# Two heads of q and k in one tile: scores as three products over the row halves of the array

## The chip, the cores and the metric

The kernel runs on one NeuronCore of a Trainium2 chip. The metric is the device time of one execution in microseconds (us), the median of several runs. The engines are TensorE (PE in the profile, its weight loads PEld), VectorE (DVE), ScalarE (ACT), GpSimd (POOL) and SyncE (SP), which issues the DMAs.

## The reference

Three stages follow each other: attention with a sigmoid in place of softmax, a Fourier mixing with an FFN, and a gated convolution with two projections. The change touches the first alone, and of it the scores.

```python
batch, n_heads, seq, head_dim = (4, 12, 448, 64)
...
scale = 1.0 / np.sqrt(q.shape[-1])
scores = scale * np.matmul(q, k.transpose(0, 1, 3, 2)) - np.log(S)
attn = 1.0 / (1.0 + np.exp(-scores))
return np.matmul(attn, v).astype(np.float32)
```

Then x = the heads side by side (4 x 448 x 768); u = x + real(fft2(x)), normalised; u + relu(un @ w_ch1) @ w_ch2; then sigmoid(causal convolution) * (x @ w_val) @ w_out. Everything is float32.

## The kernel before

**Scores in two parts.** q and k are split into an upper part of fewer mantissa bits (`qh`; F32R, a rounded float32 that TensorE takes in one pass) and the rest (`ql`). The scores of a head are (kh + kl)(qh + ql) or that without kl ql. D = 64 rows are only half of the array's 128, so before, a tile `ks` holds kh in one half of its rows and kl in the other, and q lies twice in its tile, in both halves; one product with `qh` and one with `ql` give all four terms. `upper` makes the upper part on VectorE (L308) or ScalarE (L310), `prep_q` and `prep_k` the rest on GpSimd (L317, L324). `ON_V = 24` says until when `upper` is on VectorE: all of batch 0, later only the k of odd heads.

**Steps.** Heads go in pairs, 6 pairs in a batch and 24 in all, and a pair in four steps, t = 4i .. 4i + 3 (s = t % 4), over 128 keys each. 448 keys are three tiles of 128 and 64 left over; in the step s = 3 the 64 left over of both heads stand in one tile of 128 columns, so it fills one score tile instead of two. The four `ks` tiles are used in turn, and the keys of odd heads are rolled by 64 with 64 zero columns beside them for that step.

**Order.** The program is written out in the order in which it is issued; each engine takes its instructions in that order. A step t issues `scores(t + 1)`, `sigmoid(t)` (ScalarE, L378), the preparation `prep(t + 6)` and loads, then pieces of background work taken from queues (the Fourier mixing of the batch before, its normalisation, the FFN's weights, which VectorE turns from float64 to float32 from L172 on and splits), then `values(t - 1)`:

```python
if s < 3:
    for h in range(2):
        hs = slice(64 * h, 64 * h + 64)
        nc.tensor.matmul(p[hs, :S], v[:, s, hs], a[:, h], start=(s == 0), stop=False)
else:
    nc.tensor.matmul(p[:, :S], v[:, s], a[:, 0], start=False, stop=True)
```

For s < 3 these are two products that each use 64 columns of the array (L390), for s = 3 one whole product (L392). `ps_s` (two buffers) holds scores, `sg` the sigmoids. L399 copies a finished pair to `acc`. The FFN and the rest (from `up` on) follow the attention stage; L745, L768 and so on are their products.

Of the kernel before, what the change touches and what calls it, by code (L numbers as in the profile page):

```python
# [7 lines left out]
F32 = mybir.dt.float32  # L8
F32R = mybir.dt.float32r
# [3 lines left out]
AF = mybir.ActivationFunctionType  # L13
ALU = mybir.AluOpType
# [29 lines left out]
W_RATE = (1.6, 0.25, 1.25)  # L44
FFN_RATE = (0.8, 2.2, 2)
PACE = 3
ON_V = 24
POOL_BATCHES = (2, 3)
ABSMAX = bass.bass_isa.ReduceOp.absmax
LEAST = 2.0 ** (896 // 8 - 127)  # L50
# [12 lines left out]
def body(tc, qd, kd, vd, w1d, w2d, cwd, wvd, wod, cdd, k12d, csd, eyed, out):  # L63
    nc = tc.nc
    V, A, P = nc.vector, nc.scalar, nc.gpsimd

    def pool(stack, name, side="left"):
        return stack.enter_context(tc.tile_pool(name=name, bufs=1, side=side))
# [219 lines left out]
    cs = fk.tile([128, 2, 2, 3, NP], F32R, name="cs")  # L288
    e16 = fk.tile([76, 2, 2, NE], F16, name="e16")
    V.memset(e16, 0.0)  # L290
    NHEAD, NHALF, NPAIR = B * H, 2 * B * H, B * NT
    raw, qk, st_of = {}, {}, {}
    kst = [wk.tile([128, 512], F32R, name=f"ks{i}") for i in range(4)]
    for i in range(4):
        P.memset(kst[i][:, (S, 0)[i % 2]:][:, :64].bitcast(F32), 0.0)
    SLOT = 1

    def load_qk(i):
        b, j, side = i // H, i % H // 2, i % 2
        k = wk.tile([64, S], F32, tag="k", bufs=3, name="k")  # L300
        q = wk.tile([128, S], F32, tag="q", bufs=3, name="q")
        nc.sync.dma_start(out=q, in_=qd[b, j, side])
        nc.sync.dma_start(out=k, in_=kd[b, j, side])
        raw[i] = q, k

    def upper(out, in_, m):
        if m != 2 and (m < ON_V or m % 4 == 3):
            V.tensor_copy(out, in_)  # L308
        else:
            A.activation(out=out, in_=in_, func=AF.Copy)  # L310

    def prep_q(i):
        q, k = raw[i]
        qh = wk.tile([128, S], F32R, tag="qh", bufs=4, name="qh")
        upper(qh, q, 2 * i)
        ql = wk.tile([128, S], F32R, tag="ql", bufs=4, name="ql")
        P.tensor_tensor(out=ql, in0=q, in1=qh.bitcast(F32), op=ALU.subtract)  # L317
        qk[i] = [qh, ql]

    def prep_k(i):  # L320
        q, k = raw.pop(i)
        ks, o = kst[i % 4], i % 2 * 64
        upper(ks[0:64, o:o + S], k, 2 * i + 1)
        (P if i > 1 else V).tensor_tensor(out=ks[64:128, o:o + S], in0=k, in1=ks[0:64, o:o + S].bitcast(F32), op=ALU.subtract)  # L324
        qk[i].append(ks)
# [10 lines left out]
    def amax_v(b, j):  # L336
        if j == 0:
            vm[b] = keep.tile([128, NT], F32, tag="vm", bufs=2, name="vm")
        amax(vraw[b, j], vm[b], j)

    def peak_v(b, k):
        vm[b] = peak_row(vm[b], "v") if k == 0 else peak_spread(vm[b]) if k == 1 else peak_max(vm[b], "v")

    def scale_v(b):
        e, i = pow2(vm[b], "v")
        st = scaled(i, 2.0 ** X_EXP, "st")
        rt = scaled(e, 2.0 ** -X_EXP, "rt")
        st_of[b] = st, rt
# [26 lines left out]
    def sigmoid(t):  # L375
        n = width(t)
        sg = wk.tile([128, 2, S], F32, tag="sg", bufs=LAG + 2, name="sg")
        A.activation(out=sg[:, :n], in_=sc.pop(t)[:, :n, :S], func=AF.Sigmoid, scale=1.0 / math.sqrt(D), bias=logb)  # L378
        sig[t] = sg

    def values(t):
        i, s = t // 4, t % 4
        b, j = i // NT, i % NT
        if s == 0:
            xps[b, j] = ps_m()
        p, v, a = xps[b, j], vraw[b, j], sig.pop(t)
# [6 lines that stand above are left out]
            vraw.pop((b, j))  # L393
# [9 lines left out]
    def fold_part(b, t):  # L403
        x = acc[b][:, :, PAD:]
        if t == 0:
            folds[b] = [fk.tile([128, 3, 4 * NE], F32, tag="pm", bufs=2, name="pm") for _ in range(2)]
        for pm, op in zip(folds[b], (ALU.add, ALU.subtract)):
            V.tensor_tensor(out=pm[:, t, :S], in0=x[:, t], in1=x[:, t + 3], op=op)
# [228 lines left out]
    def prep(m):
        (prep_k if m % 2 else prep_q)(m // 2)

    for i in range(2):  # L640
        load_qk(i)
        prep(2 * i)
        prep(2 * i + 1)
# [87 lines left out]
    hs = {}  # L731
# [146 lines left out]
    for part, n in blocks:  # L878
        g, b = n // B, n % B
# [77 lines left out]
    for t in range(NV + AHEAD):  # L957
        i = t + 2
# [95 lines left out]
```

## Time and profile before

| | |
|---|---|
| median of 3 runs | 1131.69 us (1129.47 to 1133.12) |
| profiled execution | 1129.11 us, span 1127.3 us |
| TensorE busy | 1076.6 us, 95% |
| VectorE busy | 787.3 us, 70% |
| ScalarE busy | 434.2 us, 39% |
| GpSimd busy | 245.2 us, 22% |
| mean granted TensorE clock | 0.986 |

Busy times are unions over the span. Matmuls are pipelined, so the records of TensorE overlap: the distance from one start to the next tells what a matmul costs, not its length. The attention stage ends at about 250 us; in it VectorE is busy nearly as long as TensorE. The clock is given as a share of 2.4 GHz.

### The profile page before, as it was taken

Reading aid. Unit: us, or ns where it says so; the run is one execution under the profiler, and the core shown is the slowest. Engines: PE = TensorE matmul, PEld = TensorE weight load, DVE = VectorE, ACT = ScalarE, POOL = GpSimd, SP = SyncE. Lnnn points to the kernel's source line nnn. Section 1 sums busy time; section 2 is a strip of 40 time slices with the busy share of each in tenths; the row PEclk is TensorE's granted clock in tenths of the full one; section 3 lists DMA queues with packets and bytes.
Section 4 is the critical chain, followed back from the end, with each engine's and each line's share of the span. In section 5 each row is a group of like instructions: output and inputs, shape, how many; then the busy total and the mean of one; then the engine's idle time right before and its main releaser. Section 6 shows DMA issues by size and latency. Waiting matters only on the chain.

```text
span 1127.3 us, 15419 instructions
## 1 busy us (share of the span) xinstructions
PE 1076.6 (95%) x5496; PEld 573.3 (51%) x5496; DVE 787.3 (70%) x2193; ACT 434.2 (39%) x666; POOL 245.2 (22%) x221
## 2 busy tenths in 40 slices
PE   9889899898989999999999999999999968999998
PEld 5446455564545555555555555555555533455554
DVE  4985999889885666667667566577664678876540
ACT  5566665843141333333233333332333323333321
POOL 5554444623420111110111111011111100000000
PEclk9999999998999999999999999999999979999999
DMA  7643343211102222233322221333221100000001
GB/s 225 193 129 99 110 134 96 79 30 36 36 15 71 57 71 62 79 85 84 85 64 77 73 72 54 85 85 85 70 72 42 44 1 0 1 33 33 33 33 66
DMA packets 38621, 78.85 MB, mean 70 GB/s; under 512 B 4708, under 2 KB 18832, under 8 KB 38544
## 3 DMA queue, kind: packets, MB, share of 16 engines
q1 hardware_dynamic: 38544, 77.87, 24.2%
q8 instruction: 43, 0.70, 0.3%
q14 instruction: 34, 0.28, 0.1%
HBM read 72.17 MB, written 5.51 MB: 69 GB/s over the span
## 4 chain that ended last, share of the span: by engine, by line
PE 76%; DVE 17%; DMA 2%; issue 2%; ACT 1%; POOL 1%; SPq 0%; ACTq 0%; POOLq 0%; DVEq 0%
PE ps_s L745 27%; PE ps_m L768 26%; PE ps_m L947 7%; PE ps_m L922 7%; PE ps_m L390 2%; PE ps_m L475 2%; DMA w<-w1d 1%; DVE gp L835 1%; PE ps_s L362 1%; DVE xm L106 1%; DVE acc L772 1%; DVE wf L199 1%; PE ps_m L492 1%; PE ps_s L363 1%; DVE wf L196 1%
## 5 line engine op out<-in xcount | busy, mean ns | idle before, releaser
L745 PE MATMUL ps_s<-un,w1hi 128*128 128x448 f16 x1152 | 316.9, 357 | 3.5 <-DVE hl L754 3.5
L745 PE MATMUL ps_s<-un,w1lo 128*128 128x448 f16 x576 | 205.5, 357 | 0.0
L768 PE MATMUL ps_m<-hh,w2hi 128*128 128x448 f16 x576 | 204.8, 356 | 0.3 <-DVE acc L772 0.3
L768 PE MATMUL ps_m<-hl,w2hi 128*128 128x448 f16 x576 | 204.4, 355 | 0.0
L768 PE MATMUL ps_m<-hh,w2lo 128*128 128x448 f16 x576 | 204.4, 355 | 0.0
L745 PEld LDWEIGHTS <-w1hi 128*128 128x128 f16 x1152 | 113.6, 99 | 111.2 <-issue 9.0
L768 PEld LDWEIGHTS <-w2hi 128*128 128x128 f16 x1152 | 113.1, 99 | 106.8 <-issue 3.9
L772 DVE SCALAR_TENSOR_TENSOR acc<-ps_m,rg,acc 128x448 f32<-128x448 f32 x192 | 129.1, 678 | 43.9 <-PE ps_m L768 43.7
L180 ACT ACTIVATE wabs<-w 128x384 f32<-128x384 f32 (+1 forms) x109 | 58.4, 548 | 207.4 <-DMA w<-w1d 69.6
L754 DVE SCALAR_TENSOR_TENSOR hl<-ps_s,hh 128x896 f16<-128x896 f32 x64 | 54.6, 854 | 94.9 <-ACT hh L752 94.9
L191 DVE TENSOR_SCALAR_CACHE_REDUCE wabs<-wabs 128x192 f32<-128x192 f32 (+1 forms) x234 | 74.5, 353 | 34.3 <-ACT wabs L180 33.2
L378 ACT ACTIVATE sg<-ps_s,logb 128x896 f32<-128x896 f32 x96 | 86.1, 912 | 26.8 <-PE ps_s L363 24.0
L752 ACT ACTIVATE hh<-ps_s 128x896 f16<-128x896 f32 x64 | 46.2, 722 | 115.3 <-PE ps_s L745 115.1
L745 PEld LDWEIGHTS <-w1lo 128*128 128x128 f16 x576 | 57.0, 99 | 54.2 <-issue 2.7
L768 PEld LDWEIGHTS <-w2lo 128*128 128x128 f16 x576 | 56.7, 98 | 53.6 <-issue 1.6
L199 DVE SCALAR_TENSOR_TENSOR wf<-w,wf 128x192 int32<-128x192 int32 (+1 forms) x234 | 82.3, 389 | 0.3
L362 PE MATMUL ps_s<-qh,ks 128*128 128x448 f32 x144 | 66.7, 463 | 13.2 <-ACT sg L378 6.9
L193 DVE TENSOR_SCALAR wf<-wabs 128x192 int32<-128x192 int32 (+1 forms) x234 | 57.5, 284 | 30.5 <-POOL w1lo L232 13.3
L196 DVE SCALAR_TENSOR_TENSOR wf<-w,wf 128x192 int32<-128x192 int32 (+1 forms) x234 | 78.5, 373 | 0.3
L922 PE MATMUL ps_m<-xs,wvhi 128*128 128x448 f16 x288 | 78.0, 352 | 0.0
L317 POOL TENSOR_TENSOR ql<-q,qh 128x448 fp32r<-128x448 f32 x48 | 59.7, 1243 | 56.6 <-ACT qh L310 29.5
L390 PE MATMUL ps_m<-sg,v 128*64 128x448 f32 x288 | 69.8, 564 | 0.0
(186 smaller groups left out, 1510.7 us busy)
## 6 DMA issues: line engine op xcount, KB each, us to landing
w<-w1d SPq DMA_DIRECT2D x42, 384.0 KB
w<-w2d SPq DMA_DIRECT2D x42, 384.0 KB
q<-qd SPq DMA_DIRECT2D x48, 224.0 KB
v<-vd SPq DMA_DIRECT2D x24, 256.0 KB
k<-kd SPq DMA_DIRECT2D x48, 112.0 KB
out<-o SPq DMA_DIRECT2D x24, 224.0 KB
w<-wvd SPq DMA_DIRECT2D x12, 384.0 KB
w<-wod SPq DMA_DIRECT2D x12, 384.0 KB
```

The source lines that it names most:

```text
L191: V.tensor_scalar(out=a, in0=a, scalar1=LEAST, scalar2=None, op0=ALU.max, op1=ALU.max, accum_out=m[:, i:i + 1])
L196: V.scalar_tensor_tensor(out=f.bitcast(I32), in0=lo, scalar=29, in1=f.bitcast(I32), op0=ALU.logical_shift_right, op1=ALU.bitwise_or)
L199: V.scalar_tensor_tensor(out=f.bitcast(I32), in0=hi, scalar=-0x40000000, in1=f.bitcast(I32), op0=ALU.bitwise_and, op1=ALU.bitwise_or)
L317: P.tensor_tensor(out=ql, in0=q, in1=qh.bitcast(F32), op=ALU.subtract)
L362: nc.tensor.matmul(p[:, h, :S], st, qh, start=True, stop=False)
L378: A.activation(out=sg[:, :n], in_=sc.pop(t)[:, :n, :S], func=AF.Sigmoid, scale=1.0 / math.sqrt(D), bias=logb)
L390: nc.tensor.matmul(p[hs, :S], v[:, s, hs], a[:, h], start=(s == 0), stop=False)
L745: nc.tensor.matmul(p[:, i, :S], w[:, k, fs], u[:, k], start=(m == 0), stop=(m == 17))
L768: nc.tensor.matmul(p[:, :S], w[:, f, js], hh[f // 2][k][:, f % 2], start=(m == 0), stop=(m == 3 * FC - 1))
L772: V.scalar_tensor_tensor(out=acc[b][:, j, PAD:], in0=p[:, :S], scalar=rg, in1=acc[b][:, j, PAD:], op0=ALU.mult, op1=ALU.add)
L922: nc.tensor.matmul(p[:, :S], w[:, k, js], u[:, k], start=(n == 0), stop=(n == 17))
L947: nc.tensor.matmul(p[:, :S], w[:, k, js], gs[b, k][i], start=(n == 0), stop=(n == 17))
```

## The change

One tile now holds q of both heads of a pair, one head in rows 0 to 63 and the other in rows 64 to 127, and another tile k of both; each has an upper part and a rest, `qh`, `ql`, `kh`, `kl`, in tiles of their own. For s < 3 the scores are three products a head, kh qh, kl qh and kh ql, over 64 rows each; the two heads of a pair stand in the two row halves of the array and write two different banks of `ps_s`. For s = 3 they are three products over all 128 rows; the host lays the 64 keys left over side by side, with zeros where a head has none. kl ql is left out. The k tile has 512 columns, q isn't doubled any more.

All four tiles of the next pair are made in steps s = 0 (q) and s = 1 (k) of a pair; the upper parts are on ScalarE but for q of the first pair and k of the first three, the rests all on GpSimd. A load of q and k is issued at s = 1, three pairs and more ahead. `ON_V`, `upper` and the four fixed `ks` tiles with their memsets go.

```diff
-    def upper(out, in_, m):
-        if m != 2 and (m < ON_V or m % 4 == 3):
-            V.tensor_copy(out, in_)
+    def halves_of(x, nm, n, on_v):
+        h = wk.tile([128, n], F32R, tag=nm + "h", bufs=2, name=nm + "h")
+        l = wk.tile([128, n], F32R, tag=nm + "l", bufs=2, name=nm + "l")
+        if on_v:
+            V.tensor_copy(h, x)
         else:
-            A.activation(out=out, in_=in_, func=AF.Copy)
+            A.activation(out=h, in_=x, func=AF.Copy)
+        P.tensor_tensor(out=l, in0=x, in1=h.bitcast(F32), op=ALU.subtract)
+        return h, l
 
     def prep_q(i):
...
+        qk[i] = halves_of(raw[i][0], "q", S, i == 0)
 
     def prep_k(i):
...
+        qk[i] += halves_of(raw.pop(i)[1], "k", 512, i < 3)
...
     def scores(t):
-        i, s = t // 4 * 2, t % 4
+        i, s = divmod(t, 4)
         p = ps_s()
-        if s < 3:
-            for h in range(2):
-                qh, ql, ks = qk[i + h]
-                st = ks[:, 128 * (s + h):128 * (s + h) + 128]
-                nc.tensor.matmul(p[:, h, :S], st, qh, start=True, stop=False)
-                nc.tensor.matmul(p[:, h, :S], st, ql, start=False, stop=True)
-        else:
-            two = qk.pop(i), qk.pop(i + 1)
-            for k in range(2):
+        qh, ql, kh, kl = qk[i]
+        cs_ = slice(128 * s, 128 * s + 128)
+        for n, (st, mv) in enumerate(((kh, qh), (kl, qh), (kh, ql))):
+            if s < 3:
                 for h in range(2):
-                    st = two[h][2][:, 384 * (1 - h):384 * (1 - h) + 128]
-                    nc.tensor.matmul(p[:, 0, :S], st, two[h][k], start=(h + k == 0), stop=(h + k == 2))
+                    hs = slice(64 * h, 64 * h + 64)
+                    nc.tensor.matmul(p[:, h, :S], st[hs, cs_], mv[hs], start=(n == 0), stop=(n == 2))
+            else:
+                nc.tensor.matmul(p[:, 0, :S], st[:, cs_], mv, start=(n == 0), stop=(n == 2))
...
-        if g == 0 and i + 5 < NHEAD:
-            load_qk(i + 5)
-        if t + 6 < NHALF:
-            prep(t + 6)
+        if t % 4 < 2 and t // 4 + 1 < NPAIR:
+            (prep_k if t % 4 else prep_q)(t // 4 + 1)
+        if t % 4 == 1 and t // 4 + 4 < NPAIR:
+            load_qk(t // 4 + 4)
```

Two places show how this moves instructions. The first is TensorE in the first two pairs, from the step s = 3 of pair 0 to the first step of pair 1. `ks_115` to `ks_118` are the tiles of four heads; "64x448 x2" are the two column halves of a value product. Before:

```order
L390 MATMUL ps_m<-sg,v 64x448 x2
L369 MATMUL ps_s<-qh,ks_115 128x448
L369 MATMUL ps_s<-qh,ks_116 128x448
L369 MATMUL ps_s<-ql,ks_115 128x448
L369 MATMUL ps_s<-ql,ks_116 128x448
L390 MATMUL ps_m<-sg,v 64x448 x2
L362 MATMUL ps_s<-qh,ks_117 128x448
L363 MATMUL ps_s<-ql,ks_117 128x448
L362 MATMUL ps_s<-qh,ks_118 128x448
L363 MATMUL ps_s<-ql,ks_118 128x448
```

and now, where "x2" on a score row are the two heads, 64 rows each:

```order
L381 MATMUL ps_m<-sg,v 64x448 x2
L358 MATMUL ps_s<-qh,kh 128x448
L358 MATMUL ps_s<-qh,kl 128x448
L358 MATMUL ps_s<-ql,kh 128x448
L381 MATMUL ps_m<-sg,v 64x448 x2
L356 MATMUL ps_s<-qh,kh 128x448 x2
L356 MATMUL ps_s<-qh,kl 128x448 x2
L356 MATMUL ps_s<-ql,kh 128x448 x2
```

The four whole products of s = 3 have become three, and the four whole products of s = 0 six of half the rows, in three rows of two.

The second place is VectorE in batch 0, where the first weights come in (`w_296` and so on are pieces of `w1d`, L183 is the first instruction that reads one). Before:

```order
L308 CAST qh<-q 128x448
L106 TENSOR_REDUCE vm<-v 128x1
L308 CAST ks_117<-k 64x448
L183 TENSOR_SCALAR wabs<-w_296 128x256
L191 TENSOR_SCALAR wabs,wm<-wabs 128x256
L193 TENSOR_SCALAR wf<-wabs 128x256
L308 CAST qh<-q 128x448
L196 SCALAR_TENSOR_TENSOR wf<-w_296,wf 128x256
L199 SCALAR_TENSOR_TENSOR wf<-w_296,wf 128x256
L308 CAST ks_118<-k 64x448
```

and now:

```order
L307 CAST kh<-k 128x512 x2
L105 TENSOR_REDUCE vm<-v 128x1
L307 CAST kh<-k 128x512
L105 TENSOR_REDUCE vm<-v 128x1
L182 TENSOR_SCALAR wabs<-w_270 128x256
L190 TENSOR_SCALAR wabs,wm<-wabs 128x256
L192 TENSOR_SCALAR wf<-wabs 128x256
L195 SCALAR_TENSOR_TENSOR wf<-w_270,wf 128x256
L198 SCALAR_TENSOR_TENSOR wf<-w_270,wf 128x256
```

Before, casts of q and k stand behind the weights' instructions and between them; now the last of them stands ahead of the first.

## Rows read from the trace of the kernel before

**Rows 1.** The page's chain of work that ended last, shares of the span by engine.

```profile
PE 76%; DVE 17%; DMA 2%; issue 2%; ACT 1%; POOL 1%; SPq 0%; ACTq 0%; POOLq 0%; DVEq 0%
```

**Rows 2.** Stretches of the attention stage: length, busy us of each engine, clock, DMA.

```profile
0.00:44.00 44.00, 38.22 (x151) 22.28 (x151) 27.67 (x57) 21.29 (x27) 24.32 (x32) 0.96 0.77 218
44.00:77.00 33.00, 28.88 (x117) 13.79 (x115) 31.74 (x66) 21.93 (x34) 20.11 (x17) 1.00 0.49 154
77.00:112.00 35.00, 35.00 (x183) 22.70 (x182) 18.41 (x38) 22.44 (x36) 16.57 (x13) 1.00 0.34 101
112.00:153.00 41.00, 35.52 (x148) 18.10 (x146) 40.21 (x85) 25.69 (x39) 18.31 (x15) 1.00 0.37 108
...
171.00:208.00 37.00, 32.34 (x149) 18.41 (x149) 36.21 (x81) 21.52 (x33) 18.31 (x15) 1.00 0.29 86
208.00:250.00 42.00, 42.00 (x223) 26.67 (x222) 34.32 (x68) 28.09 (x41) 17.43 (x14) 1.00 0.12 33
```

The engines in rows 2 are, in this order, PE, PEld, DVE, ACT and POOL.

**Rows 3.** TensorE in order of time, one pair: start us, length us, instruction.

```profile
14.20 0.37 PE L363 MATMUL ps_s<-ql,ks 128*128 128x448 f32 x1
14.50 0.97 PE L390 MATMUL ps_m<-sg,v 128*64 128x448 f32 x4
15.40 0.47 PE L362 MATMUL ps_s<-qh,ks 128*128 128x448 f32 x1
15.71 0.36 PE L363 MATMUL ps_s<-ql,ks 128*128 128x448 f32 x1
...
16.11 0.37 PE L363 MATMUL ps_s<-ql,ks 128*128 128x448 f32 x1
16.32 0.92 PE L392 MATMUL ps_m<-sg,v 128*128 128x448 f32 x2
...
17.27 0.36 PE L363 MATMUL ps_s<-ql,ks 128*128 128x448 f32 x1
...
22.71 0.47 PE L362 MATMUL ps_s<-qh,ks 128*128 128x448 f32 x1
```

**Rows 4.** Groups of instructions, 0 to 250 us: count, busy us, mean ns; idle.

```profile
L390 PE MATMUL ps_m<-sg,v 128*64 128x448 f32 x288 | 69.8, 564 | 0.0
...
L317 POOL TENSOR_TENSOR ql<-q,qh 128x448 fp32r<-128x448 f32 x48 | 59.7, 1243 | 56.6 <-ACT qh L310 29.5 <-DVE qh L308 11.1 <-DMA sp<-acc 3.3
L324 POOL TENSOR_TENSOR ks<-k,ks 64x448 fp32r<-64x448 f32 x46 | 56.5, 1227 | 46.8 <-issue 27.3 <-PE ps_s L369 7.6 <-POOL ql L317 6.4
...
L392 PE MATMUL ps_m<-sg,v 128*128 128x448 f32 x48 | 23.0, 561 | 0.0
L310 ACT ACTIVATE qh<-q 128x448 fp32r<-128x448 f32 x37 | 21.3, 576 | 6.7 <-DMA q<-qd 3.3 <-issue 2.7 <-PE ps_s L369 0.8
```

A whole float32 product leaves two records, so x48 are 24 products, and a step with two column halves leaves four.

**Rows 5.** Weight loads in order of time, the first two of a score step.

```profile
15.40 0.19 PEld L362 LDWEIGHTS ps_s<-qh,ks 128*128 128x128 f32 x1 [0.70 <-issue]
15.51 0.19 PEld L363 LDWEIGHTS ps_s<-ql,ks 128*128 128x128 f32 x1
```

**Rows 6.** Two stretches, for the instructions of L308, then L317, then L324 alone.

```profile
112.00:153.00 41.00, 1.51 (x4) 1.00 0.37 108
171.00:208.00 37.00, 1.13 (x3) 1.00 0.29 86
...
sum 78.00, POOL 16.25; mean POOL 8.12
...
sum 78.00, DVE 0.00 POOL 18.28; mean DVE 0.00 POOL 9.14
```

**Rows 7.** Two lines of VectorE: count, shortest/median/longest ns, first and last start.

```profile
L456 DVE COPY eo<-r x8: 150/978/1105, 70.7 to 261.4; 12x2 f32<-12x2 f32 x8
...
L308 DVE CAST ks<-k x30: 373/378/1335, 4.6 to 225.3; 64x448 fp32r<-64x448 f32 x30
```

**Rows 8.** Waits of TensorE, 0 to 250 us: total us, times, longest us.

```profile
PE ps_s L362 <- POOL ks L324: 5.0, 4, 3.3
```

**Rows 9.** VectorE in order of time, in brackets the idle time before it.

```profile
27.41 0.29 DVE L183 TENSOR_SCALAR wabs<-w 128x256 int32<-128x256 int32 x1 [5.97 <-DMA w<-w1d]
```

**Rows 10.** ScalarE in order of time.

```profile
135.93 0.67 ACT L261 ACTIVATE e<-eo,st 12x452 f16<-12x452 f32 x1 [4.91 <-DVE eo L428]
```

More of the change, by code (lines that the diff above doesn't have):

```diff
@@ L46 @@
 PACE = 3
-ON_V = 24
 POOL_BATCHES = (2, 3)
@@ L290, in body @@
     V.memset(e16, 0.0)
-    NHEAD, NHALF, NPAIR = B * H, 2 * B * H, B * NT
+    NHALF, NPAIR = 2 * B * H, B * NT
     raw, qk, st_of = {}, {}, {}
-    kst = [wk.tile([128, 512], F32R, name=f"ks{i}") for i in range(4)]
-    for i in range(4):
-        P.memset(kst[i][:, (S, 0)[i % 2]:][:, :64].bitcast(F32), 0.0)
     SLOT = 1
     def load_qk(i):
-        b, j, side = i // H, i % H // 2, i % 2
-        k = wk.tile([64, S], F32, tag="k", bufs=3, name="k")
+        b, j = divmod(i, NT)
+        k = wk.tile([128, 512], F32, tag="k", bufs=3, name="k")
         q = wk.tile([128, S], F32, tag="q", bufs=3, name="q")
-        nc.sync.dma_start(out=q, in_=qd[b, j, side])
-        nc.sync.dma_start(out=k, in_=kd[b, j, side])
+        nc.sync.dma_start(out=q, in_=qd[b, j])
+        nc.sync.dma_start(out=k, in_=kd[b, j])
         raw[i] = q, k
-    def upper(out, in_, m):
-        if m != 2 and (m < ON_V or m % 4 == 3):
-            V.tensor_copy(out, in_)
-        else:
-            A.activation(out=out, in_=in_, func=AF.Copy)
+    def halves_of(x, nm, n, on_v):
[3 more added lines that the diff above has]
+            V.tensor_copy(h, x)
+        else:
+            A.activation(out=h, in_=x, func=AF.Copy)
+        P.tensor_tensor(out=l, in0=x, in1=h.bitcast(F32), op=ALU.subtract)
+        return h, l
     def prep_q(i):
[L313 to L318, printed above, removed]
-    def prep_k(i):
[L321 to L325, printed above, removed]
+        qk[i] = halves_of(raw[i][0], "q", S, i == 0)
+    def prep_k(i):
+        qk[i] += halves_of(raw.pop(i)[1], "k", 512, i < 3)
     vraw = {}
@@ L355, in scores @@
     def scores(t):
-        i, s = t // 4 * 2, t % 4
+        i, s = divmod(t, 4)
         p = ps_s()
-        if s < 3:
-            for h in range(2):
-                qh, ql, ks = qk[i + h]
-                st = ks[:, 128 * (s + h):128 * (s + h) + 128]
-                nc.tensor.matmul(p[:, h, :S], st, qh, start=True, stop=False)
-                nc.tensor.matmul(p[:, h, :S], st, ql, start=False, stop=True)
-        else:
-            two = qk.pop(i), qk.pop(i + 1)
-            for k in range(2):
-                for h in range(2):
-                    st = two[h][2][:, 384 * (1 - h):384 * (1 - h) + 128]
-                    nc.tensor.matmul(p[:, 0, :S], st, two[h][k], start=(h + k == 0), stop=(h + k == 2))
+        qh, ql, kh, kl = qk[i]
+        cs_ = slice(128 * s, 128 * s + 128)
+        for n, (st, mv) in enumerate(((kh, qh), (kl, qh), (kh, ql))):
+            if s < 3:
+                for h in range(2):
+                    hs = slice(64 * h, 64 * h + 64)
+                    nc.tensor.matmul(p[:, h, :S], st[hs, cs_], mv[hs], start=(n == 0), stop=(n == 2))
+            else:
+                nc.tensor.matmul(p[:, 0, :S], st[:, cs_], mv, start=(n == 0), stop=(n == 2))
+        if s == 3:
+            qk.pop(i)
         sc[t] = p
@@ L634, in norm @@
         normed.add(b)
[L637 to L643, printed above, removed]
+    load_qk(0)
+    prep_q(0)
+    prep_k(0)
     load_v(0, 0)
+    load_qk(1)
+    load_v(0, 1)
     load_qk(2)
-    load_v(0, 1)
     load_qk(3)
-    prep(4)
-    prep(5)
-    load_qk(4)
     nc.sync.dma_start(out=eye, in_=eyed)
@@ L987 @@
     hs = np.array(heads).ravel()
-    keys = np.roll(np.arange(S), 64)
-    k = np.concatenate([k[:, hs[0::2], None], k[:, hs[1::2], None][:, :, :, keys]], axis=2).reshape(k.shape)
-    kd = k.transpose(0, 1, 3, 2).reshape(B, NT, 2, D, S)
-    qd = q[:, hs].transpose(0, 1, 3, 2)
-    qd = np.concatenate([qd, qd], axis=2).reshape(B, NT, 2, 128, S)
+    kd = np.zeros((B, NT, 2, D, 512), np.float32)
+    kt = k[:, hs].transpose(0, 1, 3, 2).reshape(B, NT, 2, D, S)
+    kd[..., :384] = kt[..., :384]
+    for h in range(2):
+        kd[:, :, h, :, 384 + 64 * h:448 + 64 * h] = kt[:, :, h, :, 384:]
+    kd = kd.reshape(B, NT, 128, 512)
+    qd = q[:, hs].transpose(0, 1, 3, 2).reshape(B, NT, 128, S)
     vf = v.transpose(0, 2, 1, 3).reshape(B, S, DM)[:, :, feats].reshape(B, S, NT, 2, D)
```

## The prediction

> **What bounds the kernel now.** I read the chain of work that ended last first: TensorE holds 76% of the span and VectorE 17% [rows 1]. The table of stretches says where the 17% lies [rows 2]. All lines that the change touches run in the attention stage, the first 250 us. Within it TensorE is busy without a gap in 77 to 112 us and in 208 to 250 us; in 112 to 153 us and 171 to 208 us it is VectorE that has no idle time (40.21 of 41 us, 36.21 of 37 us), and TensorE lacks 5.5 and 4.7 us. In 0 to 44 us and 44 to 77 us TensorE lacks 5.8 and 4.1 us. So the attention stage has two limits in turn, and an edit is worth what it takes from the one that holds at that place.
>
> Next TensorE's order of time for one pair of heads [rows 3]. Score matmuls follow each other every 0.20 us (two from 15.71 to 16.11). A pair repeats from 15.40 to 22.71, in 7.31 us: 16 score matmuls, 3.2 us; the value products, about 0.75 us for each of four; and the rest, 1.1 us, is paid where the array goes from whole products to column halves and back. From 14.20 to 15.71 such a block of halves stands between score matmuls, 1.51 us; from 16.11 to 17.27 the same work stands there as a whole product (L392), 1.16 us. In and out thus cost 0.35 us together, 0.175 us for each change of form.
>
> **The change on TensorE.** Before, a step with s < 3 is four whole matmuls: 0.80 us. After, it is three slots, in each of which the upper and the lower 64 rows of the array work for one head each. Whether the two halves run side by side is not to be seen here for rows. For columns it is: 288 records of half products fill 69.8 us, so a step with two halves fills 0.97 us, and a whole product of the same kind 0.96 us (23.0 us for 24) [rows 4]. That bounds a slot at 0.20 us from below; if the halves did not overlap at all, it would be 0.40 us. Each slot also needs two weight loads instead of one; two loads start 0.11 us apart [rows 5], so if they go one after the other they need 0.22 us a slot. I take 0.21 us, near the column halves.
>
> The step with s = 3 goes from four matmuls to three: -0.20 us. The changes of form grow from 6 to 8 in a pair, because the whole product L392 now has half-row steps on both sides: +0.35 us. A pair then costs 3 x (0.63 - 0.80) - 0.20 + 0.35 = -0.36 us (slot 0.20: -0.45; slot 0.40: +1.35; in general 9 x slot - 2.25).
>
> There is a rule that speaks against the full gain. The Trainium skill ("TensorE: Matmul & The Clock Gate", Part 3, on packing small matmuls) has row tiles running concurrently, but measured 3.07 times for four of them, not four times. An estimate from that page: a slot of 0.20 x 4/3.07 = 0.26 us, a pair at +0.09 us, and nothing left of TensorE's term. No row here shows row halves; the column halves pay nothing of the kind, so I keep 0.21 and put an incomplete overlap among the rivals.
>
> Of the 24 pairs, 7 fall into the two stretches that VectorE sets: there it casts one k a pair, four and three times [rows 6]. The other 17 are at TensorE's pace: 17 x 0.36 = **6.1 us**.
>
> **The change on VectorE and GpSimd.** In the two VectorE stretches these seven casts go (L308, 1.51 + 1.13 = 2.6 us) [rows 6]; ScalarE makes them now, within one copy for the pair. GpSimd's subtractions there are L317 and L324, 16.25 + 18.28 = 34.5 us [rows 6]. A pair now has two of them instead of four, one of them 512 wide: at the means of 1.24 us and 1.23 x 512/448 = 1.40 us [rows 4], 7 x 2.64 = 18.5 us. So 16 us of GpSimd's work leave.
>
> This matters for VectorE, because its instructions stretch beside GpSimd's: copies of 12 x 2 elements (L456) take 150 ns at the shortest and 978 ns in the median, and casts of one shape (L308) 373 to 1335 ns [rows 7]. The rows give no share, so bounds: 0 us comes back, or all 16. L456 stretches nearly always, L308's median (378 ns) hardly ever; I take half, 8 us. With the casts that is **10.6 us** in the two stretches. TensorE would be the limit there after 5.5 + 4.7 + 7 x 0.36 = 12.7 us, so the 10.6 fit in below it.
>
> The Trainium skill ("SBUF — State Buffer", Who interferes with whom) says that the port VectorE and GpSimd share is locked for a whole instruction, and that the other one blocks until it is over. The stretched L456 rows agree. By that rule alone the relief would lie nearer 16 us, and TensorE's 12.7 us would be the limit.
>
> In 0 to 44 us the largest wait of TensorE is one of 3.3 us for GpSimd's L324 [rows 8]. Its root is a queue: VectorE sat 5.97 us before L183 for a weight's DMA, and behind L183 stand the casts of q and k that GpSimd and TensorE need [rows 9]. After the change only four such casts are on VectorE, all ahead of the first L183; the others are on ScalarE, which waits for no weight in this stretch. The wait goes, and the half clock behind it (granted 0.96 over 44 us: 1.8 us) too: **5.1 us** (0 to 5.1). In 44 to 77 us TensorE's 4.1 us of gaps are VectorE's lateness again (31.74 of 33 us busy); casts leave there too, and GpSimd's work is halved as above: **4.1 us** (0 to 4.1).
>
> **Costed at nothing.** ScalarE gets all copies but four: one of 448 and one of 512 a pair, against three narrower ones after batch 0, so it is relieved there; in 0 to 44 us it has 21.29 of 44 us of work and takes some seven copies of about 0.6 us more [rows 4]. The DMAs fall, by the tiles' shapes, from 672 to 480 KB a pair, and a load now stands about eleven steps ahead of its copy, four before. The wait on SP's queue is for a k buffer that GpSimd's subtraction of the same step frees; behind it stand the v load and the weights, both due a pair later. After 250 us nothing is changed; the work left there starts earlier by what attention gained.
>
> **Sum.** 6.1 + 10.6 + 5.1 + 4.1 = 25.9 us. The profiled execution took 1129.1 us (span 1127.3), so 1103.2; it lies 2.6 us under the median of the runs, 1131.7. On the median: 1131.7 - 25.9 = **1106 us**.
>
> **Rivals.**
> *A, VectorE keeps its stretches.* If nothing comes back from GpSimd's lighter load, the two stretches give 2.6 us, and 44 to 77 us gives perhaps half: 6.1 + 2.6 + 5.1 + 2 = 16 us, 1116 us. For it: L308's median does not stretch. Against it: L456's does.
>
> *B, slower: the row halves take turns.* At 0.40 us a slot a pair costs +1.35 us. At 17 pairs that is +23 us, less the 9.2 us of waits that go in the first two stretches; in VectorE's stretches 7 x 1.35 = 9.5 us just fill TensorE's gaps of 10.2, -0.7. Together +13 us, 1145 us. It decides from 24 x (9 x slot - 2.25) = 9.2 + 10.2, a slot of 0.34 us. For it: no row of this trace has half-row matmuls. Against it: the column halves.
>
> *C, the halves come late.* Before, the first head of the next pair was prepared a pair ahead; now all four tiles of a pair are made in the two steps at its predecessor's start, behind the sigmoids. Where ScalarE stands still for VectorE (4.91 us before 135.93 [rows 10]) the copies stand behind it, then two subtractions of about 1.2 us each on GpSimd, and the scores are due two steps later, about 3.7 us at 7.31 us a pair. That could cost 2 to 3 us at each of the three places where a batch begins, 8 us in all: 1113 us. Against it: the second head's k had the same lead before.
>
> *D, the halves overlap in part.* Midway between 0.20 and the 0.34 of B, at 0.27 us, a pair costs +0.18 us: 17 x 0.18 = +3.1 us; the VectorE stretches give up to 10.2 - 7 x 0.18 = 8.9 us and the first two 9.2: -15 us, 1117 us. For it: six loads and six matmuls where there were four of each. Against it: loads 0.11 us apart, and column halves that cost as one. The packing figure of the Trainium skill's page named above would put the slot here.
>
> **Chances.** Forecast 0.58, A 0.13, B 0.14, C 0.07, D 0.08. The likeliest case alone spans from a slot of 0.20 with TensorE's limit reached everywhere (17 x 0.45 + 10.2 + 7 x 0.45 + 9.2 = 30 us, 1102; with free changes of form 24 x 0.35 = 8 us more, 1093) to a slot of 0.22 with a third of the relief (25.9 - 1.5 - 2.7 = 21.7 us, 1110). For 8 in 10 the range takes A, C and D in and leaves B out: 1092 to 1126. One measurement tells about 0.3%, 3.4 us, from no change. Faster 0.82: the forecast, A, C and D, less 0.04 for D and B meeting near a slot of 0.34; within 0.3% those 0.04; slower 0.14.
>
> **What would show it.** Two score matmuls of one slot starting within some 10 ns and slots 0.20 to 0.22 us apart; a pair at about 6.95 us in place of 7.31; L390 unchanged. No wait of TensorE over 1 us between 20 and 44 us. L456's median well under 978 ns. GpSimd's subtractions near 24 x 2.64 = 63 us in all, the attention stage over near 224 us instead of 250. I am wrong if the slots stand 0.34 us or more apart, if VectorE is as full in the two stretches and they are as long, or if TensorE waits for the new tiles at a batch's start.

## The result

The changed kernel takes **1113.94 us** (median of 4 runs, 1111.38 to 1114.73), the kernel before 1131.62 us in the same rounds (1129.47 to 1133.12): a ratio of 0.9841, 95% interval 0.9821 to 0.9860. It is 1.6% faster, 17.7 us. The forecast was 1106 us, 25.7 us less than before, with a range of 1092 to 1126.

Everything comes from the attention stage. These are the starts of ScalarE's copy of a finished pair to `acc`, for pairs 3, 7, 10, 14, 16, 19 and 23 (the last one), in the kernel before:

```profile
44.35 0.55 ACT L399 ACTIVATE acc<-ps_m 128x448 f32<-128x448 f32 x1 [1.60 <-PE ps_m L392]
...
78.93 0.54 ACT L399 ACTIVATE acc<-ps_m 128x448 f32<-128x448 f32 x1 [0.54 <-PE ps_m L392]
...
113.10 0.54 ACT L399 ACTIVATE acc<-ps_m 128x448 f32<-128x448 f32 x1 [4.70 <-PE ps_m L392]
...
153.98 0.54 ACT L399 ACTIVATE acc<-ps_m 128x448 f32<-128x448 f32 x1
...
179.63 0.55 ACT L399 ACTIVATE acc<-ps_m 128x448 f32<-128x448 f32 x1 [3.86 <-PE ps_m L392]
...
208.62 0.52 ACT L399 ACTIVATE acc<-ps_m 128x448 f32<-128x448 f32 x1
...
248.86 0.54 ACT L399 ACTIVATE acc<-ps_m 128x448 f32<-128x448 f32 x1 [3.35 <-PE ps_m L392]
```

and in the changed kernel:

```profile
39.73 0.54 ACT L390 ACTIVATE acc<-ps_m 128x448 f32<-128x448 f32 x1
...
71.58 0.55 ACT L390 ACTIVATE acc<-ps_m 128x448 f32<-128x448 f32 x1 [1.50 <-PE ps_m L383]
...
105.54 0.55 ACT L390 ACTIVATE acc<-ps_m 128x448 f32<-128x448 f32 x1 [4.89 <-PE ps_m L383]
...
139.82 0.55 ACT L390 ACTIVATE acc<-ps_m 128x448 f32<-128x448 f32 x1
...
165.29 0.54 ACT L390 ACTIVATE acc<-ps_m 128x448 f32<-128x448 f32 x1 [4.01 <-PE ps_m L383]
...
192.10 0.52 ACT L390 ACTIVATE acc<-ps_m 128x448 f32<-128x448 f32 x1
...
231.43 0.54 ACT L390 ACTIVATE acc<-ps_m 128x448 f32<-128x448 f32 x1 [3.04 <-PE ps_m L383]
```

The differences of the two lists give the gain by stretch: 4.6 us up to pair 3, 2.7 more up to pair 7, 0.2 to pair 10, 6.6 to pair 14, 0.2 to pair 16, 2.2 to pair 19 and 0.9 to pair 23, 17.4 us in all. The two profiled executions differ by 15.5 us only: what follows the last copy, where nothing is changed, took 878.4 us before and 880.4 after, and between 878.4 and 881.6 us in all the kernels below. The two stretches that VectorE sets (pairs 10 to 14 and 16 to 19, cut at the copies) gave half, 8.8 us; the places behind pair 7 where TensorE sets the pace gave 1.3 us.

The table of stretches, moved by these gains (columns as in [rows 2]):

```profile
0.00:38.00 38.00, 33.29 (x170) 16.83 (x172) 13.90 (x34) 20.76 (x30) 12.45 (x18) 1.00 0.68 216
38.00:69.00 31.00, 27.57 (x140) 11.24 (x138) 25.97 (x65) 22.07 (x33) 10.64 (x8) 1.00 0.50 146
69.00:104.00 35.00, 34.65 (x199) 18.96 (x197) 17.68 (x43) 20.96 (x32) 8.41 (x7) 1.00 0.33 98
104.00:139.00 35.00, 33.08 (x171) 15.01 (x170) 33.60 (x73) 24.07 (x35) 9.76 (x7) 1.00 0.36 107
...
157.00:191.00 34.00, 30.09 (x165) 14.48 (x163) 33.21 (x77) 19.36 (x28) 9.59 (x8) 1.00 0.28 83
191.00:232.00 41.00, 40.81 (x237) 23.44 (x238) 31.84 (x65) 28.05 (x41) 12.41 (x10) 1.00 0.05 14
```

GpSimd's share has halved (9.76 us where there were 18.31). VectorE still has no idle time to speak of in 104 to 139 us and 157 to 191 us (33.60 of 35, 33.21 of 34), but these stretches are shorter. In the first two stretches of the table, 0 to 69 us, TensorE still lacks 4.7 and 3.4 us.

TensorE in order of time, from the first score step of one pair to that of the next, and at pair 7, where a block of the Fourier mixing (L466) follows a step of row halves ("x2" are the two heads):

```profile
13.56 0.48 PE L356 MATMUL ps_s<-qh,kh 64*128 64x448 f32 x2
13.88 0.36 PE L356 MATMUL ps_s<-qh,kl 64*128 64x448 f32 x2
14.07 0.37 PE L356 MATMUL ps_s<-ql,kh 64*128 64x448 f32 x2
...
20.46 0.48 PE L356 MATMUL ps_s<-qh,kh 64*128 64x448 f32 x2
20.77 0.36 PE L356 MATMUL ps_s<-qh,kl 64*128 64x448 f32 x2
20.98 0.37 PE L356 MATMUL ps_s<-ql,kh 64*128 64x448 f32 x2
...
71.99 0.37 PE L356 MATMUL ps_s<-ql,kh 64*128 64x448 f32 x2
72.28 1.03 PE L466 MATMUL ps_m<-cd,ph 128*113 128x385 f16 x5
```

Two products of 64 rows fill one slot of 0.19 to 0.21 us (13.88 to 14.07, 20.77 to 20.98), and the pair repeats after 6.90 us (13.56 to 20.46), 0.41 less than before [rows 3]. The block L466 starts 0.29 us after the last score product; before it was 0.20 us:

```profile
79.32 0.36 PE L363 MATMUL ps_s<-ql,ks 128*128 128x448 f32 x1
79.52 0.66 PE L475 MATMUL ps_m<-cd,ph 128*113 128x385 f16 x3
```

Two waits are new or longer: ScalarE's copies of `cs` (constants of the Fourier mixing, loaded as `cst`) stand still for a DMA, with sigmoids behind them, which they didn't before; and SP's queue waits longer for GpSimd. First ScalarE in order of time:

```profile
23.39 0.52 ACT L260 ACTIVATE cs<-cst 128x384 fp32r<-128x384 f32 x1 [2.18 <-DMA cst<-csd]
...
36.51 0.52 ACT L260 ACTIVATE cs<-cst 128x384 fp32r<-128x384 f32 x1 [2.96 <-DMA cst<-csd]
36.94 0.62 ACT L369 ACTIVATE sg<-ps_s,logb 128x448 f32<-128x448 f32 x1
```

then what TensorE waits for there:

```profile
25.29 0.47 PE L358 MATMUL ps_s<-qh,kh 128*128 128x448 f32 x1 [1.29 <-ACT sg L369]
...
37.61 0.47 PE L356 MATMUL ps_s<-qh,kh 64*128 64x448 f32 x2 [1.81 <-ACT sg L369]
```

and the waits of SP's queue in 0 to 110 us (total, times, longest), for the loads of k and q:

```profile
SPq L300 <- POOL kl L310: 30.4, 11, 6.6
SPq L299 <- POOL ql L310: 26.1, 9, 4.7
```

In the kernel before the same two took 34.4 us:

```profile
SPq L303 <- POOL ks L324: 19.8, 18, 2.9
SPq L302 <- POOL ql L317: 14.6, 14, 3.1
```

In the part up to pair 7 the two lines grew less: 16.4 us in 0 to 77 us before, 22.4 in 0 to 69 us now.

### The profile page after: what moved, and what is told of

Read it like the earlier page. It is cut to its first block, busy times and chain, and to the rows that moved or that the text cites. A ratio compares the mean times of both kernels' runs of the same rounds, so it can differ in the third digit from the quotient of the medians.

```text
span 1111.8 us, 15303 instructions
## 1 busy us (share of the span) xinstructions
PE 1066.1 (96%) x5616; PEld 550.7 (50%) x5616; DVE 756.1 (68%) x2154; ACT 427.7 (38%) x654; POOL 191.1 (17%) x171
## 4 chain that ended last, share of the span: by engine, by line
PE 76%; DVE 16%; DMA 3%; ACT 3%; issue 1%; POOL 1%; SPq 0%; ACTq 0%; DVEq 0%; POOLq 0%
PE ps_s L730 26%; PE ps_m L753 26%; PE ps_m L932 7%; PE ps_m L907 7%; DMA w<-w1d 3%; PE ps_m L466 2%; PE ps_m L381 2%; PE ps_s L356 2%; PE ps_m L483 1%; DVE gp L820 1%; DVE wf L195 1%; DVE wf L198 1%; DVE xm L105 1%; DVE acc L757 1%; DVE wabs L190 1%
## 5 line engine op out<-in xcount | busy, mean ns | idle before, releaser
L190 DVE TENSOR_SCALAR_CACHE_REDUCE wabs<-wabs 128x192 f32<-128x192 f32 (+1 forms) x234 | 74.6, 353 | 35.9 <-ACT wabs L179 35.1
L369 ACT ACTIVATE sg<-ps_s,logb 128x896 f32<-128x896 f32 x96 | 86.3, 913 | 26.7 <-PE ps_s L356 22.4
L198 DVE SCALAR_TENSOR_TENSOR wf<-w,wf 128x192 int32<-128x192 int32 (+1 forms) x234 | 78.1, 371 | 0.3
L195 DVE SCALAR_TENSOR_TENSOR wf<-w,wf 128x192 int32<-128x192 int32 (+1 forms) x234 | 77.0, 366 | 0.4
L804 DVE SCALAR_TENSOR_TENSOR gp<-acc,cw,gp 128x448 f32<-128x448 f32 x72 | 49.3, 685 | 25.0 <-ACT gp L802 23.1
L932 PE MATMUL ps_m<-gh,wolo 128*128 128x448 f16 x144 | 50.8, 352 | 0.0
```

The source lines that it names most:

```text
L190: V.tensor_scalar(out=a, in0=a, scalar1=LEAST, scalar2=None, op0=ALU.max, op1=ALU.max, accum_out=m[:, i:i + 1])
L195: V.scalar_tensor_tensor(out=f.bitcast(I32), in0=lo, scalar=29, in1=f.bitcast(I32), op0=ALU.logical_shift_right, op1=ALU.bitwise_or)
L198: V.scalar_tensor_tensor(out=f.bitcast(I32), in0=hi, scalar=-0x40000000, in1=f.bitcast(I32), op0=ALU.bitwise_and, op1=ALU.bitwise_or)
L932: nc.tensor.matmul(p[:, :S], w[:, k, js], gs[b, k][i], start=(n == 0), stop=(n == 17))
```

## Theory, rivals and experiments

**Theory.** GpSimd's lighter load is the gain, because VectorE's instructions stretch beside it; the shorter pairs of TensorE add little; and the loads of the first 77 us took a part back. **Rivals:** TensorE's shorter pairs are the gain; or it is the casts that left VectorE. The times of the twelve runs stand here, with GpSimd's busy time of the whole span, the two stretches (pairs 10 to 14 and 16 to 19, added) worked out from the pair copies of each trace, and GpSimd's busy time within these two. Each ratio is to the kernel before in the same rounds, whose medians were 1130.5 to 1131.6 us.

| kernel | median us | ratio to before, 95% | GpSimd us | two stretches us | GpSimd in them us |
|---|---|---|---|---|---|
| before | 1131.6 | | 245.2 | 69.9 | 34.9 |
| after | 1113.9 | 0.9821 to 0.9860 | 191.1 | 61.1 | 18.9 |
| e1 heads in turn | 1113.8 | 0.9821 to 0.9863 | 192.6 | 60.7 | 20.1 |
| e7 both heads in one half | 1141.1 | 1.0064 to 1.0113 | 190.3 | 66.2 | 20.4 |
| e3 before, no `ql` | 1115.2 | 0.9837 to 0.9872 | 185.1 | 61.4 | 18.6 |
| e6 before, casts moved | 1132.0 | 0.9996 to 1.0021 | 245.1 | 69.9 | 35.1 |
| e12 e3 and e6 | 1115.4 | 0.9834 to 0.9890 | 185.2 | 61.3 | 18.8 |
| e4 after, k on VectorE | 1112.0 | 0.9794 to 0.9857 | 191.0 | 60.2 | 17.8 |
| e2 after, subtractions twice | 1139.0 | 1.0040 to 1.0082 | 257.4 | 70.8 | 38.6 |
| e9 e2 with four buffers | 1131.8 | 0.9993 to 1.0018 | 257.6 | 70.5 | 38.1 |
| e8 after, four buffers | 1112.1 | 0.9811 to 0.9856 | 191.7 | 61.1 | 18.9 |
| e5 after, `cs` later | 1113.1 | 0.9817 to 0.9855 | 190.3 | 61.1 | 18.8 |
| e10 e8 and e5 | 1109.1 | 0.9785 to 0.9830 | 191.3 | 61.1 | 18.9 |
| e13 e10, no `ql` | 1103.7 | 0.9741 to 0.9777 | 162.6 | 56.1 | 12.2 |

In all of these but e7 VectorE has at most 1.5 us without work in the two stretches together; in e7 it is TensorE that has none (66.24 us busy).

The last column's first and second figure are read from these sums, before and after:

```profile
sum 69.87, PE 59.05 PEld 30.16 DVE 68.39 ACT 46.14 POOL 34.94; mean PE 29.53 PEld 15.08 DVE 34.20 ACT 23.07 POOL 17.47
```

```profile
sum 61.09, PE 55.26 PEld 24.15 DVE 59.61 ACT 43.04 POOL 18.87; mean PE 27.63 PEld 12.07 DVE 29.80 ACT 21.52 POOL 9.44
```

### Do the row halves run side by side, and does their order matter?

e1 writes one head's three products and then the other's:

```diff
-        for n, (st, mv) in enumerate(((kh, qh), (kl, qh), (kh, ql))):
-            if s < 3:
-                for h in range(2):
-                    hs = slice(64 * h, 64 * h + 64)
+        terms = tuple(enumerate(((kh, qh), (kl, qh), (kh, ql))))
+        if s < 3:
+            for h in range(2):
+                hs = slice(64 * h, 64 * h + 64)
+                for n, (st, mv) in terms:
```

> The changed kernel with the order of the six half-row products of a step turned: three of one head, then three of the other, so that neighbours stand in the same row half. If the gain rests on two halves that work side by side, a step goes from three slots of 0.20 us to about six matmuls of 0.20 us, a pair from 6.9 to 8.7 us; 17 pairs at TensorE's pace give 31 us, the rest of the stage some 7 more, less up to 8 us of waits of TensorE that are filled: about 1114 + 32 = 1146 us, slower than the kernel before. If the order does not matter (the array takes the other half ahead), 1114 us.

e7 leaves the program as it is and puts both heads on the same 64 rows:

```diff
-                    hs = slice(64 * h, 64 * h + 64)
+                    hs = slice(0, 64)
```

> The changed kernel, with both heads' products of 64 rows put on rows 0 to 63 (it computes the first head's scores twice and leaves the second head's out). Number, shape and order of the instructions are the same; only the side by side of two row halves is gone. If the halves' overlap is what makes a slot 0.20 us, a slot becomes 0.40, a pair 1.8 us longer (9 slots), 24 pairs 43 us, less up to 15 us of gaps that TensorE now has in the attention stage: 1140 to 1157 us. Rival: a product over 64 rows costs half a whole one by itself, or the weight loads set the slot: 1112 to 1116 us, slots still near 0.20.

e1 costs nothing: 1113.75 us. Its TensorE in order of time shows why; although three products of one head stand ahead of the other's first in the program, that first one starts with the other head's first (one group, x2, 0.48 us long as a single product is):

```profile
20.64 0.48 PE L357 MATMUL ps_s<-qh,kh 64*128 64x448 f32 x2
20.95 0.37 PE L357 MATMUL ps_s<-qh,kl 64*128 64x448 f32 x2
21.15 0.37 PE L357 MATMUL ps_s<-ql,kh 64*128 64x448 f32 x2
```

By the single records the two starts lie 10 ns apart in the median, 3 ns in the changed kernel. The trace keeps the times and not the order of issue, so that the array itself takes the other half ahead is the plain reading of the program's text, and not shown apart. Either way e1 could not price a lost overlap. e7 does, on the same view:

```profile
21.59 0.67 PE L356 MATMUL ps_s<-qh,kh 64*128 64x448 f32 x2
22.11 0.57 PE L356 MATMUL ps_s<-qh,kl 64*128 64x448 f32 x2
22.52 0.57 PE L356 MATMUL ps_s<-ql,kh 64*128 64x448 f32 x2
```

A slot is 0.41 us now (22.11 to 22.52), and the pair copies stand 8.72 us apart in place of 6.90. The rival that 64 rows are cheap by themselves, or that the weight loads set the slot, falls: shape and number of both are those of the changed kernel. Without the overlap the change would have lost 9.8 us against before.

### GpSimd's load, with either form of the products

e3 takes the kernel before, and lets the products with `ql` read `qh`, so that half of GpSimd's subtractions go and nothing else (the terms with `ql` are left out):

```diff
-        ql = wk.tile([128, S], F32R, tag="ql", bufs=4, name="ql")
-        P.tensor_tensor(out=ql, in0=q, in1=qh.bitcast(F32), op=ALU.subtract)
-        qk[i] = [qh, ql]
+        qk[i] = [qh, qh]
```

> The kernel before without the rest of q: its product is made with the upper part again, so that 48 of GpSimd's 94 subtractions go (60 us) while TensorE, VectorE's casts and the DMAs stay. This leaves out the terms with ql. If GpSimd's load costs VectorE time, 5 to 10 us: 1122 to 1127 us; and the wait of 3.3 us for GpSimd's k near 32 us shrinks by one subtraction, about 1 us. If only TensorE's pace counts: 1131 us.

e2 takes the changed kernel and does each subtraction twice, the second time into a tile that nothing reads:

```diff
         P.tensor_tensor(out=l, in0=x, in1=h.bitcast(F32), op=ALU.subtract)
+        d = wk.tile([128, n], F32R, tag="d", bufs=2, name="d")
+        P.tensor_tensor(out=d, in0=x, in1=h.bitcast(F32), op=ALU.subtract)
```

> The changed kernel with each subtraction on GpSimd done a second time into a tile that nothing reads, so that GpSimd's work on q and k is about 122 us, as before, and nothing else is new. If lighter GpSimd work is what shortened the stretches in which VectorE is full, these grow again: 112 to 154 us took 6.6 us less after the change, 44 to 77 us and 171 to 208 us some 2 to 3 less each, and 5 to 9 us of it come back: 1119 to 1123 us. If TensorE's shorter pairs made the whole gain, nothing happens: 1114 us.

e3 gained more than expected, 16.4 us of the change's 17.7, and e2 lost more, 25 us. e2 mixes two causes, since a late GpSimd also frees the raw tiles later, on which SP's queue waits. e9 is e2 with four buffers for raw q and k (and one for `d`); e8 is the changed kernel with four.

```diff
-        k = wk.tile([128, 512], F32, tag="k", bufs=3, name="k")
-        q = wk.tile([128, S], F32, tag="q", bufs=3, name="q")
+        k = wk.tile([128, 512], F32, tag="k", bufs=4, name="k")
+        q = wk.tile([128, S], F32, tag="q", bufs=4, name="q")
```

> The doubled subtractions of the earlier run with four raw buffers, so that a late GpSimd no longer holds SP's queue. If the 25 us of that run came by the queue (loads and weights late), most goes: 1112 to 1122 us. If they came by VectorE stretching beside GpSimd and by GpSimd being late itself, they stay: 1132 to 1140 us.

> The changed kernel with four buffers instead of three for the raw q and k tiles, so that a load on SP's queue takes the buffer of a pair whose subtraction is long over. Theory: SP's waits for GpSimd (56.5 us for kl and ql in 0 to 110 us) hold back the weights, v and cst behind them; these waits nearly go, VectorE's idle time for weights falls from 18 us to near 8, and the time to 1108 to 1112 us. Rival, the wait costs nothing as the prediction had it: 1113 to 1115 us.

With the queue free 19.7 us of the loss stay (e9 against e8), and 7.2 us go (e9 against e2). e9 has the new products and four casts on VectorE in place of 41, but GpSimd is busy again (257.6 us, 12.4 more than before), and it takes the time of before: 1131.8 against 1131.3 us in the same rounds. Its two stretches are those of before too, 70.5 against 69.9 us. The granted clock in them was 0.96 and 0.95, where it was 1.00 before; VectorE, though, was busy in 69.0 of the 70.5 us. The stretching is seen in one group of VectorE, the last step of the weights' split. Before, after, in e9 and in e13 (the last run below), in this order (mean ns behind the comma):

```profile
L199 DVE SCALAR_TENSOR_TENSOR wf<-w,wf 128x256 int32<-128x256 int32 x18 | 13.8, 764 | 0.3
```

```profile
L198 DVE SCALAR_TENSOR_TENSOR wf<-w,wf 128x256 int32<-128x256 int32 x18 | 9.6, 533 | 0.3
```

```profile
L198 DVE SCALAR_TENSOR_TENSOR wf<-w,wf 128x256 int32<-128x256 int32 x18 | 13.6, 755 | 0.3
```

```profile
L198 DVE SCALAR_TENSOR_TENSOR wf<-w,wf 128x256 int32<-128x256 int32 x18 | 8.5, 474 | 0.3
```

### The casts

e6 takes the kernel before and moves the casts of batch 0 to ScalarE, but for those of heads 0 to 2 (`m` counts two casts a head; "heads 0 to 5" in its expectation is a slip); e12 makes that edit and e3's together; e4 takes the changed kernel and puts all upper parts of k back on VectorE.

```diff
-        if m != 2 and (m < ON_V or m % 4 == 3):
+        if m != 2 and (m < 6 or m % 4 == 3 and m > 24):
```

```diff
-        qk[i] += halves_of(raw.pop(i)[1], "k", 512, i < 3)
+        qk[i] += halves_of(raw.pop(i)[1], "k", 512, True)
```

> The kernel before, with the casts of q and k of batch 0 on ScalarE but for those of heads 0 to 5 (later batches as they are). The prediction's reading of the first 44 us: TensorE's wait of 3.3 us for GpSimd comes from casts queued behind weights on VectorE; then this edit alone removes it, the copy to acc of pair 3 starts 3 to 5 us earlier than 44.35 us, and the time is 1125 to 1128 us. Rival, GpSimd's load sets it: the wait stays in some form, 1130 to 1133 us.

> The kernel before with the same move of batch 0's casts and with the subtractions of q left out (its products with ql take qh, so those terms are missing): the preparation is about as light as in the changed kernel, TensorE's products are those of before. If the preparation is the whole gain: 1111 to 1114 us. If TensorE's shorter pairs carry 4 us or more of it: 1116 us or more, that is no better than the 1115 us of halving the subtractions alone.

> The changed kernel with the upper parts of k on VectorE in all 24 pairs instead of the first three (21 casts of 128x512, 0.4 to 0.7 us each, 8 to 15 us of VectorE in all, 7 of them in its two full stretches, 3 to 5 us). If VectorE sets those stretches still: 1117 to 1121 us. Rival, ScalarE's copies are what holds the pairs up now: 1110 to 1114 us.

e6 gains nothing, as its rival had it: by its pair copies pair 2 comes 4.3 us earlier (32.70 us for 36.95), but pair 3 at 45.12, 0.8 us later. The wait has moved on by a pair. Now ScalarE waits for a load of q, with a sigmoid behind it (ScalarE's wait, then TensorE's):

```profile
39.91 0.58 ACT L310 ACTIVATE qh<-q 128x448 fp32r<-128x448 f32 x1 [4.42 <-DMA q<-qd]
...
41.73 0.74 PE L362 MATMUL ps_s<-qh,ks 128*128 128x448 f32 x1 [3.53 <-ACT sg L378]
```

The trace tells why that load is late. SP's queue stands from 25.99 us on before it issues a weight (L172) at 33.14, 1.8 us of it for another weight's DMA and 5.4 for VectorE's work on that one, and the load of q goes out behind it, at 34.47. e6 leaves the casts in the two stretches where they were; those are e4's test.

e12, between its two cases, is no better than e3. e4 has the time of its rival and isn't slower than the changed kernel (1109.55 to 1113.01 us), and its two stretches are no longer, although 21 casts, 9.6 us, came back to VectorE, five of them, 3.0 us, in these two. VectorE's busy time rose by 2.2 us only, 756.1 to 758.3; why its other work got 7 us shorter stays open, and so does the reason that the rival gave (ScalarE's copies).

### The loads of the first 77 us

e5 puts ScalarE's copies of `cst` later, and their last two loads:

```diff
-        if b == 0 and r in (5, 6, 10, 11):
-            c, o = divmod((5, 6, 10, 11).index(r), 2)
+        if b == 0 and r in (5, 6, 13, 14):
+            c, o = divmod((5, 6, 13, 14).index(r), 2)
...
-        if b == 0 and r in (8, 9, 14, 15):
-            c, o = divmod((8, 9, 14, 15).index(r), 2)
+        if b == 0 and r in (12, 13, 17, 18):
+            c, o = divmod((12, 13, 17, 18).index(r), 2)
```

> The changed kernel with ScalarE's four copies of the Fourier constants (cs) moved from steps 8, 9, 14 and 15 of the first batch to 12, 13, 17 and 18, the last two loads to 13 and 14. After the change ScalarE stands 2.18, 2.96 and 0.39 us for their DMA, with the sigmoids behind it, and TensorE waits 1.3 and 1.8 us for these. If that is where part of the expected gain in the first 44 us went, 3 us come back: 1111 us. If the weights' DMA or VectorE holds the stage there anyway, the wait appears at the next one and it is 1114 us.

e10 makes the edits of e5 and of e8.

> Four raw buffers and the copies of cst on ScalarE three to seven steps later (steps 12, 13, 17, 18 instead of 8, 9, 14, 15). With the queue free cst should land in time, so both of the first stretches' new waits go: 1105 to 1110 us by the theory that these waits are what the change gave back in the first 77 us. Rival, VectorE's load sets the first 77 us too, whatever waits: 1111 to 1114 us.

In e5 the wait only moved (ScalarE waits 3.39 us for `cst` before 41.40 us): 1113.1 us. e8 took most of SP's wait for kl and ql away, 56.5 to 10.4 us:

```profile
SPq L300 <- POOL kl L310: 9.0, 7, 2.7
...
SPq L299 <- POOL ql L310: 1.4, 1, 1.4
```

but its queue now stands 37.9 us at the load of v, and 1112.1 us is not told apart from 1113.9. The two edits together are: all four runs of e10 (1108.05 to 1110.87) lie below all four of the changed kernel. Pair 7 is copied at 67.99 us there, 71.58 in the changed kernel, 70.49 in e5 and 68.85 in e8, so by the one trace of each the buffers give most of it. One wait for `cst`, 1.98 us before 40.06 us, is left, and a sigmoid behind it.

### What is left in VectorE's stretches

e13 is e10 without the subtractions of q.

```diff
+        if nm == "q":
+            return h, h
+        l = wk.tile([128, n], F32R, tag=nm + "l", bufs=2, name=nm + "l")
         P.tensor_tensor(out=l, in0=x, in1=h.bitcast(F32), op=ALU.subtract)
```

> The changed kernel with four raw buffers and late copies of cst (the run of 1109 us), its 24 subtractions of q left out (products with ql take qh, those terms are missing; TensorE, VectorE's program and all loads stay): about 29 us of GpSimd's 191 us go. Theory: VectorE beside GpSimd still sets the two full stretches; at 0.38 us of VectorE per us of GpSimd (22.9 of 60.1 us and 25.3 of 65.9 us in the earlier runs) VectorE's busy time falls by 11 us and the time to 1102 to 1106 us. Rival, TensorE and the loads set it all by now: 1108 to 1110 us.

The theory held: 5.4 us less than e10. The page's busy times, e10 first and then e13:

```profile
PE 1065.1 (96%) x5616; PEld 550.7 (50%) x5616; DVE 754.4 (68%) x2154; ACT 427.5 (39%) x654; POOL 191.3 (17%) x171
```

```profile
PE 1063.0 (97%) x5616; PEld 550.1 (50%) x5616; DVE 740.7 (67%) x2154; ACT 427.9 (39%) x654; POOL 162.6 (15%) x147
```

GpSimd lost 28.7 us, and VectorE, whose program is the same, 13.7 us. In the first of the two stretches TensorE now has no gap either (31.88 of 31.88 us busy).

## Why the prediction was right, and where its terms were off

By the prediction's own terms, with the 24 pairs dealt out to the stretches: up to pair 7 it had 5.1 + 4.1 + 8 x 0.36 = 12.1 us; VectorE's two stretches 10.6; the nine other pairs 9 x 0.36 = 3.2. Measured: 7.3, 8.8 and 1.3 us. The direction and the range held; of the sum of 25.9 us 8.5 are missing, and each part has its own reason. The time alone, 1113.9 us, lies nearer to the rivals A, C and D (1116, 1113 and 1117 us) than to the forecast; that the forecast's mechanism holds is told by the stretches and the runs. The range was drawn to take these three in, so that it held says little by itself.

**The pair on TensorE: right.** A slot is 0.20 to 0.21 us (0.21 was taken), the pair 6.90 us (6.95). Rivals B and D fall with it; e7 shows B's price, 9.8 us slower than before, where the prediction had +13. By the packing figure that the Trainium skill gives ("TensorE: Matmul & The Clock Gate", Part 3), a slot was estimated at 0.26 us; two halves here show no such loss.

**17 pairs x 0.36 us: too large.** The step counted changes of form within a pair only. Where background work follows a step of row halves, one more change is paid: 0.29 us to the first matmul where it was 0.20, as the rows of L466 show. In the single records of pairs 8 to 10 five blocks pay this 0.09 us, their first two matmuls stand 0.05 us (L466, three blocks) or 0.10 us (L483, two) further apart than behind a whole step, and one score step waits 0.35 us for a sigmoid: about 1.1 us of the 1.2 that three pairs 0.41 us shorter would save. They saved 0.2. With GpSimd's load lowered in both, new products against old gave 1.3 us (e3 against after), 3.1 with four buffers (e8), and neither is clear of noise: the intervals of the ratios overlap. At the heavy load nothing is seen (e9), but GpSimd has 12.4 us more to do there than before, which at half a microsecond each can hide 6 us.

**"I take half": right; the casts, 2.6 us: wrong.** In VectorE's two stretches, cut at the copies, the change took GpSimd from 34.9 to 18.9 us and gave 8.8 us: 0.55 us for each. e3 took it to 18.6 and gave 8.5: 0.52; doubling took it from 18.9 (e8) to 38.1 (e9) and cost 9.4: 0.49; e13 took it from 18.9 (e10) to 12.2 and gave 5.0: 0.75. That is half three times; why the last step gave more stays open. The prediction's half was a choice between bounds, and no row had pointed to it. Nothing is left for the casts: e3, with all of them, is 0.3 us short of the change, and e4 loses nothing. Rival A falls. The lock rule of the Trainium skill ("SBUF — State Buffer", Who interferes with whom), taken for every instruction of VectorE, which is wider than that section has it, would have brought the relief nearer the whole 16 us; the runs show half. L447, the small copy, has a median of 854 ns, not "well under 978"; the weights' L198 shows the relief, 764 to 533 ns.

**The first 77 us: the edits costed at nothing.** Two of them were not. SP's wait for GpSimd, "behind it stand the v load and the weights, both due a pair later", grew from 34.4 to 56.5 us (in this part from 16.4 to 22.4); and `cst` came too late for ScalarE, which had been taken for an engine with room. The half clock did go (granted 1.00 in 0 to 38 us), but TensorE's wait of 3.3 us went only in part: sigmoids behind `cs` took its place. e10 gives 3.6 us of that back, and stands at 10.9 of the 12.1 us forecast for this part. The reading of the root was only half of it. With the casts taken away pair 2 does come 4.3 us earlier (e6), but the wait comes back a pair later at a load of q, which stands in SP's queue behind a weight that VectorE is late to read. No run moved that load apart, so what it costs stays open.

Rival C is not seen: TensorE's products wait for `kl` once, for 0.2 us, and its weight loads four times, 1.2 us in all; attention gained at every batch's start.

## What to carry to other kernels

Where VectorE is the limit, look at what GpSimd does beside it: here a microsecond of elementwise work taken from GpSimd gave half a microsecond of VectorE's stretch or more, while putting the casts back on VectorE cost nothing that was seen. When an edit takes an engine's wait away, follow the loads behind it: whoever is next in line for a DMA, and whichever queue that DMA stands in, becomes the wait. And count changes of the array's form at every neighbour of the changed products, the background work between them too.

## What the runs showed of the hardware

Products on different row halves do not keep the program's order among each other: in e1 a head's first product starts within 10 ns of the other head's first, past two that stand ahead of it in the program's text, and the kernel's time doesn't tell the two orders apart (1113.75 and 1113.94 us). Whether the array or an earlier step changes the order isn't shown. Products on the same half do follow each other, 0.20 us apart (e7: two in 0.41 us). Leaving a step of row halves for a product over the whole array cost 0.09 us more than leaving a whole product (0.29 against 0.20 us from start to start). Elementwise subtractions on GpSimd stretch VectorE's instructions beside them: one group of 18 took 764 ns each with four subtractions a pair, 533 with two, 755 with the two made twice and 474 with one.
